# Tile 0's softmax in two parts of its keys, and the first three tiles' operations in one written list

## The chip, the cores and the metric

The kernel runs on one core of a Trainium2 chip. The metric is the device time of one execution, in microseconds (us). The engines work through queues of their own, in the order in which the program gives them work, and wait for each other by semaphores: PE (TensorE, matmuls), DVE (VectorE), ACT (ScalarE), POOL (GpSimd), and SP, whose queue issues every DMA here.

## The reference

```python
kv_pool = kv.reshape(B, H // r, r, W // r, r, C).mean(axis=(2, 4))   # r = 4
kv_flat = kv_pool.reshape(B, -1, C) @ w_sr                           # 768 keys, k = v
s = scale * (q @ k.transpose(0, 2, 1))
a = softmax(s)                       # over the keys, exp(s - max) / (sum + 1e-9)
x = a @ v                            # (B * 12288, 128)
h = x @ w_in                         # 128 -> 2048
out = gelu(h) @ w_out                # 2048 -> 128, gelu by erf
```

There are four batches (B) of 12,288 queries, C is 128, and q is eight times the usual draw. `w_in` and `w_out` come as 64-bit floats.

## The kernel before

The 49,152 queries are cut into 96 tiles of T = 512, 24 to a batch; a tile's queries are four chunks of 128. For a tile t the steps are:

- `q_load`, `q_max`, `q_scale`, `q_split` (or `q_halves`), `q_turn`: q is loaded, scaled by a power of two for each row, split into two f16 halves (upper and remainder), and transposed by DMA (`q_u` to `q_v`). `q_sigma` makes the factor `sg` that undoes the scale.
- `score`, `evac`, `exp`: for each chunk, six f16 matmuls of 384 columns give the 768 scores in PSUM (`s`, line 478); VectorE copies them out with the row's extreme (`sn`, line 489); ScalarE takes the exponential with its sum (line 540).
- `recips`, `attn_hi`, `attn_lo`, `attn_turn`: the reciprocal of the sum (`r`), the upper half and remainder of the normalized row (`a`, lines 561 and 565), and a DMA transpose (`aT`, line 574).
- `av`, `x_out`: 18 matmuls of 512 columns give x transposed (`px`, line 600), which VectorE splits into `xh` and `xl`.
- `mlp_in`, `gelu`, `rest`, `mlp_out`: 16 blocks of 128 of the hidden layer: three matmuls (`h`, lines 622 to 624), the gelu on ScalarE (`g`, line 635), its upper half for a pair of blocks on ScalarE (`gh`, line 637) and the remainder on VectorE (`gl`, line 643), three matmuls into `po` (lines 660 to 662). `ps_h`, with three PSUM banks, holds `h` and every small product.
- `o_turn`, `o_join`: the output is turned back by a DMA transpose between two copies on GpSimd, and stored.

Tile 0 is another matter: its keys, softmax and MLP are in f32, where one matmul instruction runs four passes. The first batch's key and value rows come in six parts (`kv_in`); VectorE adds neighbours twice (`kv_add`), a matmul with `pool32` pools and turns (`kv_pool`, `pp`), a matmul with `w_sr` gives the keys (`kv_key`, `pk`) and the values (`kv_nat`, `pv`). Its scores are two halves of 384 keys for each chunk (`score_half`, `evac_half`), but there is one exponential over all 768, one normalization (`norm`, line 445), six transposes on PE for a chunk (`a_turn`, `pa`) with their copies shared by ScalarE and VectorE (`a_evac`, line 461), and `av_pair`, 12 matmuls of 256 columns that give x transposed (`px`, line 586), copied by `x_first` into `x32`.

Beside this the weights are made ready: `w_load` brings 64-bit floats, `w_single` makes f32 of them by four integer passes, of which one is ScalarE's (line 719), `w_max` and `w_scale` find the scale (`rho`, `omega`; a product with `ones` spreads it over the partitions), and `w_half` writes f16 halves (`wi_h` and the like on ScalarE, line 784, `wi_l` and the like on VectorE, line 786).

The order on every engine is the order in which the code calls the steps (`tc.manual_schedule`). `START` is a list of calls, 52 lines long, for the preparation and tile 0, with the parts of tiles 1 and 2 that lie beside it. After it a loop over tile i and block f calls the steps of tiles i to i + 3 at fixed places, and `extra` puts the later batches' keys among them.

Of the kernel before, what the change touches and what calls it, by code (L numbers as in the profile page):

```python
# [20 lines left out]

START = [
    ("q_load", 0), ("w_sr",), ("kv_in", 0), ("kv_in", 1), ("kv_in", 2), ("kv_in", 3), ("kv_in", 4),
    ("kv_in", 5, 0, 2), ("kv_in", 5, 1, 2), ("q_load", 1), ("w_load", 0, 0, 2), ("w_load", 0, 1, 2),
    ("w_load", 1), ("w_load", 2), ("w_load", 3), ("q_load", 2),
    ("q_turn_first",),
    ("kv_add", 0), ("kv_pool", 0), ("kv_key", 0), ("kv_add", 1), ("kv_pool", 1), ("kv_key", 1),
    ("kv_add", 2), ("kv_pool", 2), ("kv_key", 2), ("kv_add", 3),
    ("score_half", 0, 0, 0), ("score_half", 0, 1, 0), ("kv_pool", 3), ("kv_key", 3),
    ("kv_max", 0), ("evac_half", 0, 0, 0), ("kv_add", 4),  # L30
    ("kv_pool", 4), ("score_half", 0, 2, 0), ("score_half", 0, 3, 0), ("kv_key", 4),
    ("evac_half", 0, 1, 0), ("kv_add", 5, 0, 2), ("kv_add", 5, 1, 2), ("kv_pool", 5), ("kv_key", 5),
    ("evac_half", 0, 2, 0), ("evac_half", 0, 3, 0), ("q_max", 1), ("q_scale", 1), ("q_halves", 1, 0),
    ("w_single", 0, 0), ("w_single", 0, 1), ("q_halves", 1, 1), ("q_turn", 1),
    ("score_half", 0, 0, 1), ("score_half", 0, 1, 1), ("score_half", 0, 2, 1),
    ("evac_half", 0, 0, 1), ("exp", 0, 0), ("score_half", 0, 3, 1),
    ("evac_half", 0, 1, 1), ("exp", 0, 1), ("kv_nat", 0),
    ("evac_half", 0, 2, 1), ("exp", 0, 2), ("recips", 0, 0, 1), ("norm", 0, "dve"),
    ("a_turn", 0, 0), ("a_turn", 0, 1), ("evac_half", 0, 3, 1), ("a_evac", 0, 0, "act"), ("exp", 0, 3),
    ("kv_max", 1), ("a_evac", 0, 1, "dve"), ("kv_bound", 0), ("kv_nat", 1),  # L40
    ("recips", 0, 1, 1), ("norm", 1, "dve"), ("kv_bound", 1), ("a_turn", 1, 0),
    ("a_turn", 1, 1), ("kv_bound", 2), ("a_evac", 1, 0, "act"), ("kv_high", 0), ("kv_high", 1), ("a_evac", 1, 1, "dve"),
    ("recips", 0, 2, 1), ("norm", 2, "dve"), ("av_pair", 0), ("a_turn", 2, 0), ("a_turn", 2, 1),
    ("kv_low", 0), ("a_evac", 2, 0, "act"), ("w_single", 1, 0),
# [34 lines left out]
def pooled_attention_mlp(  # L79
# [14 lines left out]
    nc = tc.nc  # L94
# [16 lines left out]
    LAG = 6  # L111

    GROUPS = H // P
    PARTS = 2 * GROUPS
    WL = 1024
# [76 lines left out]
    def kv_add(h, n=0, parts=1):  # L192


        v = st["row", h].rearrange("p (j w c) -> p j w c", w=R, c=C)
        v = v[:, n * 4 // parts : (n + 1) * 4 // parts]
        nc.vector.tensor_tensor(v[:, :, :2], v[:, :, :2], v[:, :, 2:], op=ALU.add)
        nc.vector.tensor_tensor(v[:, :, 0], v[:, :, 0], v[:, :, 1], op=ALU.add)

    def kv_pool(h):  # L200


        v = st["row", h].rearrange("p (j w c) -> p j w c", w=R, c=C)
        ps = ps_h.tile([P, T], F32, tag="ps_h", name=f"pp_{h}")
        for j in range(4):
            nc.tensor.matmul(  # L206
                ps[:, j * P // 4 : (j + 1) * P // 4], v[:, j, 0], pool32, start=True, stop=True
            )
        if h == 0:
            st["pT"] = ap_.tile([P, PARTS, P], F32, tag="a", name="pT")  # L210
        nc.scalar.copy(st["pT"][:, h], ps[:, :P])

    def kv_nat(n):


        if n == 0:
            st["v32"] = ap_.tile([P, KB, C], F32, tag="a", name="v32")
        ps = ps_h.tile([P, T], F32, tag="ps_h", name=f"pv_{n}")
        for k in range(3):
            nc.tensor.matmul(  # L220
                ps[:, k * C : (k + 1) * C], st["pT"][:, 3 * n + k], w_sr_sb, start=True, stop=True
            )
        nc.scalar.copy(
            st["v32"][:, 3 * n : 3 * n + 3].rearrange("p k c -> p (k c)"), ps[:, : 3 * C]
        )

    def kv_key_first(h):
        if h == 0:
            st["kT", 0] = prep.tile([P, KEYS], F32, tag="kT", name="kT_0")
        ps = ps_h.tile([P, T], F32, tag="ps_h", name=f"pk_{h}")  # L230
        nc.tensor.matmul(ps[:, :P], w_sr_sb, st["pT"][:, h], start=True, stop=True)
        nc.scalar.copy(st["kT", 0][:, h * P : (h + 1) * P], ps[:, :P])
# [138 lines left out]
    def q_max(t):  # L371

        st["qm", t] = small.tile([P, CH], F32, tag="qm", name=f"qm_{t}")
        nc.vector.tensor_reduce(
            st["qm", t], st["q", t], axis=AX.X, op=ALU.max, apply_absolute_value=True
        )

    def q_scale(t):

        m = st.pop(("qm", t))  # L380
        st["qe", t] = small.tile([P, CH], I32, tag="qe", name=f"qe_{t}")
        st["qi", t] = small.tile([P, CH], I32, tag="qi", name=f"qi_{t}")
# [17 lines left out]
    def q_halves(t, step):  # L400


        x = st["q", t]
        if step == 0:
            st["qu", t] = qs.tile([P, 2, CH, C], F16, tag="u", name=f"q_{t}_u")
        u, i = st["qu", t], st["qi", t].bitcast(F32)
        for c in range(CH):
            if step == 0:
                nc.scalar.mul(u[:, 0, c], x[:, c], i[:, c : c + 1])
            else:  # L410
                nc.vector.scalar_tensor_tensor(
                    u[:, 1, c], x[:, c], i[:, c : c + 1], u[:, 0, c],
                    op0=ALU.mult, op1=ALU.subtract,
                )
        if step == 1:
            del st["q", t], st["qi", t]
# [517 lines left out]
```

## Time and profile before

| what | value |
|---|---|
| runs | 2820.65, 2822.84, 2825.28 us (median 2822.84) |
| the profiled execution | 2821.22 us |
| its span on the core | 2819.5 us |
| PE, ACT, DVE, POOL busy | 2780.0, 2518.4, 2366.3, 847.0 us |
| mean granted TensorE clock | 0.997 |

A busy PE means that a matmul was under way, not that it ran at its peak. A row of groups has the number of instructions behind an x, then their busy time together in us and the mean of one in ns, and behind the second bar the idle time of the engine just before them and who ended it. A timeline row has the start, the time taken, the engine, the line, the operation, what it writes and reads, and in brackets the wait before it and its releaser. A window row has its bounds and length, then the busy time and the number of instructions for PE, its weight loads (PEld), DVE, ACT and POOL, the granted clock, the share of the DMA engines and GB/s. An f32 matmul shows as two records.

### The profile page before, as it was taken

What the parts mean: (1) busy time and instruction counts of PE and PEld (TensorE: products, weight loads), DVE (VectorE), ACT (ScalarE), POOL (GpSimd) and SP (SyncE); (2) the same over time, 40 slices, a digit from 0 to 9 for tenths busy, and PEclk for the clock granted to TensorE, in tenths of its full rate; (3) what the DMA queues carried; (4) which work ended last, traced back from release to release, by engine and by line L of the source; (5) the groups of instructions that cost most, each with busy time, mean ns of one, the idle gap of its engine ahead of it and who ended that gap; (6) DMA issues with size and microseconds to landing.
All of it is one profiled execution on the core that took longest, in us unless ns stands there. A gap on an engine that the chain in (4) does not pass through costs nothing.

```text
span 2819.5 us, 37507 instructions
## 1 busy us (share of the span) xinstructions
PE 2780.0 (99%) x13384; PEld 1329.3 (47%) x13384; DVE 2366.3 (84%) x3494; ACT 2518.4 (89%) x3411; POOL 847.0 (30%) x795
## 2 busy tenths in 40 slices
PE   7799999999999999999999999999999999999999
PEld 4344444444444444444444444444444444444444
DVE  7788888898888888888888888889888888888885
ACT  4699899999999999989999999999999989999997
POOL 0243442222243444222223434332322222222221
PEclk9899999999999999999999999999999999999999
DMA  5344543343445444434344444434443434343431
GB/s 184 89 103 113 118 112 90 94 99 92 96 103 122 109 108 102 98 86 103 90 97 120 107 106 106 111 92 93 97 96 89 93 90 97 90 97 90 95 90 48
DMA packets 844764, 283.05 MB, mean 100 GB/s; under 512 B 807200, under 2 KB 809632, under 8 KB 843808
## 3 DMA queue, kind: packets, MB, share of 16 engines
q1 hardware_dynamic: 844576, 280.65, 42.3%
q8 instruction: 105, 1.72, 0.3%
q14 instruction: 83, 0.68, 0.1%
HBM read 54.59 MB, written 25.17 MB: 28 GB/s over the span
## 4 chain that ended last, share of the span: by engine, by line
PE 95%; DVE 2%; ACT 1%; DMA 1%; POOL 1%; issue 1%; SPq 0%; DVEq 0%; ACTq 0%; POOLq 0%
PE s L478 13%; PE px L600 12%; PE po L661 11%; PE po L660 11%; PE po L662 11%; PE h L622 11%; PE h L624 11%; PE h L623 11%; DVE a L565 0%; PE po L654 0%; DMA q_v<-q_u 0%; DVE gl L643 0%; PE pp L206 0%; ACT sn L540 0%; DVE a L561 0%
## 5 line engine op out<-in xcount | busy, mean ns | idle before, releaser
L635 ACT ACTIVATE g<-h,hs 128x512 f32<-128x512 f32 x1520 | 995.3, 680 | 213.4 <-PE h L624 169.8
L643 DVE SCALAR_TENSOR_TENSOR gl<-g,gs,gh 128x1024 f16<-128x1024 f32 x760 | 1004.2, 1334 | 27.0 <-ACT gh L637 18.1
L637 ACT ACTIVATE gh<-g,gs 128x1024 f16<-128x1024 f32 x760 | 872.7, 1148 | 24.8
L660 PE MATMUL po<-gh,wo_h 128*128 128x512 f16 x1520 | 576.1, 379 | 1.7 <-ACT oT L667 1.7
L395 POOL TENSOR_TENSOR q<-q,qi 128x512 f32<-128x512 f32 x93 | 96.9, 1042 | 1599.7 <-DVE qi L387 1359.5
L661 PE MATMUL po<-gl,wo_h 128*128 128x512 f16 x1520 | 576.1, 379 | 0.4 <-DVE gl L643 0.4
L624 PE MATMUL h<-xh,wi_l 128*128 128x512 f16 x1520 | 576.3, 379 | 0.0
L623 PE MATMUL h<-xl,wi_h 128*128 128x512 f16 x1520 | 576.3, 379 | 0.0
L622 PE MATMUL h<-xh,wi_h 128*128 128x512 f16 x1520 | 576.3, 379 | 0.0
L662 PE MATMUL po<-gh,wo_l 128*128 128x512 f16 x1520 | 576.1, 379 | 0.0
L489 DVE TENSOR_SCALAR_CACHE_REDUCE sn<-s,sg 128x768 f32<-128x768 f32 x380 | 384.7, 1012 | 79.6 <-PE s L478 79.0
L478 PE MATMUL s<-k,q_v 128*128 128x384 f16 x2280 | 434.6, 327 | 14.3 <-DMA q_v<-q_u 7.5
L565 DVE SCALAR_TENSOR_TENSOR a<-sn,r,a 128x768 f16<-128x768 f32 x380 | 407.7, 1073 | 14.2 <-ACT a L561 0.8
L600 PE MATMUL px<-aT,v 128*128 128x512 f16 x1710 | 415.3, 379 | 0.0
L540 ACT ACTIVATE sn<-sn,nm 128x768 f32<-128x768 f32 x384 | 354.5, 924 | 1.2
L478 PEld LDWEIGHTS <-q_v 128*128 128x128 f16 x2280 | 223.3, 98 | 206.6 <-issue 13.0
L600 PEld LDWEIGHTS <-v 128*128 128x128 f16 x1710 | 167.3, 98 | 201.7
L561 DVE TENSOR_SCALAR a<-sn,r 128x768 f16<-128x768 f32 x378 | 248.4, 657 | 6.8 <-DVE r L557 0.3
L553 DVE TENSOR_SCALAR r<-sum 128x2 f32<-128x2 f32 (+1 forms) x193 | 40.8, 211 | 252.6 <-ACT sn L540 252.6
L369 POOL COPY o<-o_v 128x512 uint16<-128x512 uint16 x190 | 153.1, 849 | 279.0 <-DMA o_v<-o_u 273.3
L662 PEld LDWEIGHTS <-wo_l 128*128 128x128 f16 x1520 | 148.7, 98 | 180.0 <-issue 0.7
L624 PEld LDWEIGHTS <-wi_l 128*128 128x128 f16 x1520 | 148.8, 98 | 179.4 <-issue 0.3
(129 smaller groups left out, 2168.9 us busy)
## 6 DMA issues: line engine op xcount, KB each, us to landing
q<-in_q_dram SPq DMA_DIRECT2D x96, 256.0 KB, 2.9
out_dram<-o SPq DMA_DIRECT2D x95, 256.0 KB, 2.0
kv<-in_kv_dram SPq DMA_DIRECT2D x72, 256.0 KB, 4.4
aT<-a SPq DMA_TRANSPOSE x380, 3.2
row<-in_kv_dram SPq DMA_DIRECT2D x5, 1024.0 KB, 10.2
w<-in_moe_w_out_dram SPq DMA_DIRECT2D x2, 1024.0 KB, 10.8
q_v<-q_u SPq DMA_TRANSPOSE x95, 2.8
o_v<-o_u SPq DMA_TRANSPOSE x95, 2.7
```

The source lines that it names most:

```text
L478: nc.tensor.matmul(ps[:, n, :KH], lhs[:, c], rhs[:, n * KH : (n + 1) * KH], start=rhs is kh and lhs is qh, stop=lhs is ql,)
L565: nc.vector.scalar_tensor_tensor(a[:, 1, :], st.pop(("s", t, c)), st["r", t][:, c : c + 1], a[:, 0, :], op0=ALU.mult, op1=ALU.subtract,)
L600: nc.tensor.matmul(ps, v[:, w, :], aT[:, :, o + k, :], start=k == 0 and i == 0, stop=k == KB - 1 and i == 2,)
L622: nc.tensor.matmul(ps, wi_h[:, fs], xh, start=True, stop=False)
L623: nc.tensor.matmul(ps, wi_h[:, fs], xl, start=False, stop=False)
L624: nc.tensor.matmul(ps, wi_l[:, fs], xh, start=False, stop=True)
L635: nc.scalar.activation(g[:, e, :], ps, AF.Gelu, scale=st["hs", b] if t > 0 else 1.0)
L637: nc.scalar.mul(st["gh", t, f // 2], g, st["gs", b])
L643: nc.vector.scalar_tensor_tensor(gl, st["g", t, p], st["gs", t // TPB], st["gh", t, p], op0=ALU.mult, op1=ALU.subtract)
L660: nc.tensor.matmul(ps, wo_h[:, f, :], gh[:, e, :], start=f == 0, stop=False)
L661: nc.tensor.matmul(ps, wo_h[:, f, :], gl[:, e, :], start=False, stop=False)
L662: nc.tensor.matmul(ps, wo_l[:, f, :], gh[:, e, :], start=False, stop=f == FB - 1)
```

## The change

It has four parts.

1. **Tile 0's softmax.** Each chunk's keys are two parts, key blocks 0 to 2 and 3 to 5 (`CUT`). Each part has its own scores, maximum, exponential with sum, transposes and value product (`score_part`, `evac_part`, `exp_part`, `turn_part`, `turn_out_part`, `av_part`). `parts` makes the factors that bring both to a common maximum and sum, and `join_first` (ScalarE) and `join_second` (VectorE) apply them to the two products. The products have the queries on the partitions (24 matmuls of 128 columns), so `x_turn` turns x on PE afterwards.
2. **Work that changes engine.** For key parts 3, 4 and 5 VectorE's second addition is left out, and PE pools both columns (8 matmuls for 4). All copies of tile 0's transposes go to ScalarE. The scale of `w_out` is found by ScalarE as a sum of absolute values (`w_sum`) in place of VectorE's maximum. The upper halves of the weights go to VectorE, and most upper halves of `a` in tiles 1 to 3 to ScalarE.
3. **Smaller ones.** Tiles 1 and 2 have one scale for the four query rows of a partition (`JOINT`), so q's halves are one instruction each. `w_single`'s first step writes into `wa` itself.
4. **The list.** `START` now holds every operation of tiles 0, 1 and 2, and those of the tiles behind that lie among them; the loop starts at i = 3, through a generator `slots(i)` that yields the same steps in the old order.

```diff
+UNROLLED = 2
 START = [
-    ("q_load", 0), ("w_sr",), ("kv_in", 0), ("kv_in", 1), ("kv_in", 2), ("kv_in", 3), ("kv_in", 4),
...
+    ("q_load", 0), ("kv_in", 1), ("kv_add", 1), ("kv_in", 0), ("kv_in", 2), ("w_sr",),
...
+    JOINT = 2
+    SINGLE = (3, 4, 5)
+    CUT = (0, 3, KB)
...
         nc.vector.tensor_tensor(v[:, :, :2], v[:, :, :2], v[:, :, 2:], op=ALU.add)
-        nc.vector.tensor_tensor(v[:, :, 0], v[:, :, 0], v[:, :, 1], op=ALU.add)
+        if h not in SINGLE:
+            nc.vector.tensor_tensor(v[:, :, 0], v[:, :, 0], v[:, :, 1], op=ALU.add)
...
+        m = 2 if h in SINGLE else 1
         for j in range(4):
+            for w in range(m):
+                nc.tensor.matmul(
+                    ps[:, j * P // 4 : (j + 1) * P // 4], v[:, j, w], pool32,
+                    start=w == 0, stop=w == m - 1,
+                )
...
+    def evac_part(c, n):
...
+        ks = slice(CUT[n] * P, CUT[n + 1] * P)
+        nc.vector.tensor_scalar(
+            st["s", 0, c][:, ks], st.pop(("s0", c, n)), -SCALE, None,
+            op0=ALU.mult, op1=ALU.min, accum_out=st["nm0"][:, n, c : c + 1],
+        )
+    def exp_part(c, n):
+        s = st["s", 0, c][:, CUT[n] * P : CUT[n + 1] * P]
+        nc.scalar.activation(
+            s, s, AF.Exp, bias=st["nm0"][:, n, c : c + 1], scale=-1.0,
+            accum_out=st["sum0"][:, n, c : c + 1],
+        )
...
+    def av_part(c, n):
...
+        ps = st["x0", n, c // 2][:, c * C : (c + 1) * C]
+        for k in range(CUT[n], CUT[n + 1]):
+            nc.tensor.matmul(
+                ps, st["a0"][:, k, c * P : (c + 1) * P], st["v32"][:, k],
+                start=k == CUT[n], stop=k == CUT[n + 1] - 1,
+            )
+    def parts(step):
+        nm, sm, d, f = (st[x] for x in ("nm0", "sum0", "d0", "f0"))
+        if step == 0:
+            nc.vector.tensor_tensor(f[:, 0], nm[:, 0], nm[:, 1], op=ALU.min)
+            nc.vector.tensor_tensor(
+                d, f[:, 0:1].to_broadcast([P, 2, CH]), nm, op=ALU.subtract
+            )
+        if step == 1:
+            nc.scalar.activation(d, d, AF.Exp)
+        if step == 2:
+            nc.vector.tensor_tensor(f, sm, d, op=ALU.mult)
...
+    def join_first(c, mul):
...
+        mul(st["y0"][:, c], st["x0", 0, c // 2][:, c * C : (c + 1) * C], st["f0"][:, 0, c : c + 1])
+    def join_second(c):
+        y = st["y0"][:, c]
+        nc.vector.scalar_tensor_tensor(
+            y, st["x0", 1, c // 2][:, c * C : (c + 1) * C], st["f0"][:, 1, c : c + 1], y,
+            op0=ALU.mult, op1=ALU.add,
+        )
...
-            nc.scalar.mul(st["wy", j], up.bitcast(F32), DOWN)
+            nc.scalar.mul(a, up.bitcast(F32), DOWN)
...
+    def w_sum(j):
...
+        nc.scalar.activation(
+            wo_hf[:, k * WL : (k + 1) * WL], wa[:, j * WL : (j + 1) * WL], AF.Abs,
+            accum_out=st["wm", i][:, k : k + 1],
+        )
...
-        for i in range(1, NT + 1):
...
+        for i in range(UNROLLED + 1, NT + 1):
+            for name, *a in slots(i):
+                by[name](*a)
```

Three places show how the order moves. The first is VectorE at the evacuation of tile 2's first scores, `sn_2_0`. (`w_3` and `w_0` are pieces of the raw weights, `wa` the f32 weights, `a_1_2` chunk 2 of tile 1's normalized rows.) Before:

```order
L557 RECIPROCAL r_1_554<-r_1_554 128x2
L721 TENSOR_SCALAR w_3_162<-w_3_162 128x1024
L565 SCALAR_TENSOR_TENSOR a_1_2_576<-sn_1_2_472,r_1_554,a_1_2_576 128x768
L565 SCALAR_TENSOR_TENSOR a_1_3_581<-sn_1_3_502,r_1_554,a_1_3_581 128x768
L723 SCALAR_TENSOR_TENSOR w_3_162<-w_3_162 128x1024
L727 SCALAR_TENSOR_TENSOR wa_134<-wy_3_477,w_3_162 128x1024
L489 TENSOR_SCALAR sn_2_0_605,nm_2_603<-s_2_0_596,sg_2_529 128x768
L489 TENSOR_SCALAR sn_2_1_618,nm_2_603<-s_2_1_611,sg_2_529 128x768
```

After:

```order
L834 TENSOR_SCALAR w_1_436<-w_1_436 128x1024
L836 SCALAR_TENSOR_TENSOR w_2_426<-w_2_426 128x1024
L504 TENSOR_SCALAR sg_2_519<-qe_2_279,ks_0_324 128x1
L676 TENSOR_SCALAR r_1_521<-sum_1_405 128x2
L679 RECIPROCAL r_1_521<-r_1_521 128x2
L659 TENSOR_SCALAR sn_2_0_526,nm_2_524<-s_2_0_494,sg_2_519 128x768
L849 TENSOR_REDUCE wm_0_544<-wa_134 128x1
L840 SCALAR_TENSOR_TENSOR wa_134<-wa_134,w_2_426 128x1024
L687 SCALAR_TENSOR_TENSOR a_1_0_534<-sn_1_0_406,r_1_521,a_1_0_534 128x768
```

Tile 2's first evacuation moves ahead of all of tile 1's normalization, and the weights' passes lie between it and the next.

The second is SP's queue at the transposes of q and of the normalized rows. Before:

```order
L329 DMA_TRANSPOSE v_0_394<-k_0_361 128x12x128
L421 DMA_TRANSPOSE q_2_v_527<-q_2_u_486 128x8x128
L348 DMA q_3_531<-in_q_dram 128x512
L574 DMA_TRANSPOSE aT_1_560<-a_1_0_557 128x12x128
L574 DMA_TRANSPOSE aT_1_560<-a_1_1_564 128x12x128
L574 DMA_TRANSPOSE aT_1_560<-a_1_2_576 128x12x128
L574 DMA_TRANSPOSE aT_1_560<-a_1_3_581 128x12x128
L421 DMA_TRANSPOSE q_3_v_706<-q_3_u_702 128x8x128
```

After:

```order
L400 DMA_TRANSPOSE v_0_430<-k_0_350 128x12x128
L817 DMA w_1_436<-in_moe_w_in_dram 128x2048
L495 DMA_TRANSPOSE q_2_v_482<-q_2_u_290 128x8x128
L821 DMA w_3_509<-in_moe_w_out_dram 128x8x256
L419 DMA q_4_532<-in_q_dram 128x512
L696 DMA_TRANSPOSE aT_1_584<-a_1_0_534 128x12x128
L495 DMA_TRANSPOSE q_3_v_616<-q_3_u_580 128x8x128
L696 DMA_TRANSPOSE aT_1_584<-a_1_1_554 128x12x128
L696 DMA_TRANSPOSE aT_1_584<-a_1_3_604 128x12x128
```

Tile 3's q moves ahead of three of tile 1's transposes, and two loads of weights, which stood ahead of `v_0`, move behind it.

The third is ScalarE around tile 0's x (`x32`, the input of `h_0_0`). Before:

```order
L317 ACTIVATE k_0_361<-kT_0_182,kinv_0_354 128x384 x2
L461 COPY aT_0_314<-pa_2_0_375 128x3x128
L719 ACTIVATE wy_1_385<-w_1_158 128x1024
L469 COPY x32_391<-px_0_0_368 128x256
L461 COPY aT_0_314<-pa_3_0_396 128x3x128
L635 ACT_TABLE_LOAD
L635 ACTIVATE g_0_0_421<-h_0_0_419 128x512
L635 ACTIVATE g_0_0_421<-h_0_1_426 128x512
```

After:

```order
L832 ACTIVATE wa_134<-w_2_426 128x1024
L617 ACTIVATE y0_417<-xa_346,f0_221 128x128
L832 ACTIVATE wa_134<-w_1_436 128x1024
L617 ACTIVATE y0_417<-xa_346,f0_221 128x128
L667 ACTIVATE sn_1_1_420,sum_1_405<-sn_1_1_420,nm_1_404 128x768
L667 ACTIVATE sn_1_0_406,sum_1_405<-sn_1_0_406,nm_1_404 128x768
L636 COPY x32_489<-px_0_0_479 128x256
L636 COPY x32_489<-px_0_1_491 128x256
L667 ACTIVATE sn_1_2_447,sum_1_405<-sn_1_2_447,nm_1_404 128x768
L741 ACT_TABLE_LOAD
L741 ACTIVATE g_0_0_514<-h_0_0_502 128x512
```

Passes over weights, joins and two of tile 1's exponentials now stand ahead of the copy of x, and a third exponential behind it, ahead of the first gelu.

More of the change, by code (lines that the diff above doesn't have):

```diff
@@ L426, in q_sigma @@
     def q_sigma(t):
-        st["sg", t] = small.tile([P, CH], F32, tag="sg", name=f"sg_{t}")
+        n = 1 if t <= JOINT else CH
+        st["sg", t] = small.tile([P, CH], F32, tag="sg", name=f"sg_{t}")[:, :n]
         nc.vector.tensor_scalar_mul(
@@ new lines, in score_part @@
+    def score_part(c, n):
+        name = f"s0_{c}_{n}"
+        if c < 2:
+            if ("ps0", n) not in st:
+                st["ps0", n] = ps_s.tile([P, 2, 512], F32, tag="ps_s", name=name)
+            ps = st["ps0", n][:, c]
+        elif n == 0:
+            pool, tag = ((ps_o, "ps_o"), (ps_t, "ps_t"))[c - 2]
+            ps = pool.tile([P, T], F32, tag=tag, name=name)
+        else:
+            ps = ps_h.tile([P, T], F32, tag="ps_h", name=name)
+        ks = slice(CUT[n] * P, CUT[n + 1] * P)
+        ps = ps[:, : ks.stop - ks.start]
+        nc.tensor.matmul(ps, st["q32"][:, c], st["kT", 0][:, ks], start=True, stop=True)
+        st["s0", c, n] = ps
@@ new lines, in evac_part @@
+    def evac_part(c, n):
+        if "nm0" not in st:
+            for x in ("nm0", "sum0", "d0", "f0"):
+                st[x] = small.tile([P, 2, CH], F32, tag=x, bufs=1, name=x)
+        if ("s", 0, c) not in st:
+            st["s", 0, c] = sp.tile([P, KEYS], F32, tag="s", name=f"sn_0_{c}")
+        ks = slice(CUT[n] * P, CUT[n + 1] * P)
+        nc.vector.tensor_scalar(
+            st["s", 0, c][:, ks], st.pop(("s0", c, n)), -SCALE, None,
+            op0=ALU.mult, op1=ALU.min, accum_out=st["nm0"][:, n, c : c + 1],
+        )
@@ L452, in attn_turn_first, with turn_part @@
+    def exp_part(c, n):
[4 more added lines that the diff above has]
+        )
+    def turn_part(c, n):
+        if "a0" not in st:
+            st["a0"] = atp.tile([P, KB, T], F32, tag="aT", name="aT_0")
         ps = ps_h.tile([P, T], F32, tag="ps_h", name=f"pa_{c}_{n}")
-        for k in range(3):
+        for k in range(CUT[n], CUT[n + 1]):
+            o = (k - CUT[n]) * P
@@ L466, in x_first @@
-    def x_first(n, copy=nc.scalar.copy):
-        if n == 0:
+            st["a0"][:, CUT[n] : CUT[n + 1], c * P : (c + 1) * P],
+            st.pop(("pa", c, n))[:, :w].rearrange("p (k t) -> p k t", t=P),
+        )
+    def av_part(c, n):
+        if n == 0 and ("x0", 0, 0) not in st:
+            st["x0", 0, 0] = ps_x.tile([P, T], F32, tag="ps_x", name="xa")
+            st["x0", 0, 1] = st["x0", 0, 0]
+        if ("x0", n, c // 2) not in st:
+            pool, tag = ((ps_t, "ps_t"), (ps_o, "ps_o"))[c // 2]
+            st["x0", 1, c // 2] = pool.tile([P, T], F32, tag=tag, name=f"xb_{c}")
+        ps = st["x0", n, c // 2][:, c * C : (c + 1) * C]
+        for k in range(CUT[n], CUT[n + 1]):
+            nc.tensor.matmul(
+                ps, st["a0"][:, k, c * P : (c + 1) * P], st["v32"][:, k],
+                start=k == CUT[n], stop=k == CUT[n + 1] - 1,
+            )
@@ L543, in exp @@
         )
-    def exps(t):
-        for c in range(CH):
-            exp(t, c)
     def recips(t, c=0, n=CH):
@@ L738, in w_max @@
             apply_absolute_value=True,
+        )
+    def w_sum(j):
+        i, k = j // NW, j % NW
+        if ("wm", i) not in st:
+            st["wm", i] = small.tile([P, NW], F32, tag=f"wm{i}", name=f"wm_{i}")
+        nc.scalar.activation(
+            wo_hf[:, k * WL : (k + 1) * WL], wa[:, j * WL : (j + 1) * WL], AF.Abs,
+            accum_out=st["wm", i][:, k : k + 1],
         )
```

604 lines of the change are left out of this document (323 added, 281 removed).

## The prediction

> **What bounds the kernel now.** I read the page's busy table and slices first, then the busy time by stretch, the timeline of the first 125 us, and the groups there for durations. All times are us from the start of the span.
>
> ```profile
> span 2819.5 us, 37507 instructions
> PE 2780.0 (99%) x13384; PEld 1329.3 (47%) x13384; DVE 2366.3 (84%) x3494; ACT 2518.4 (89%) x3411; POOL 847.0 (30%) x795
> PE   7799999999999999999999999999999999999999
> ```
>
> Only the first two slices (141 us) are not full on PE: no later edit of order can win much, and the change touches only the head. By stretch:
>
> ```profile
> 0.00:45.70 45.70, 30.51 (x143) 23.89 (x143) 30.57 (x74) 17.08 (x38) 1.33 (x10) 1.00 0.76 263
> 45.70:121.04 75.34, 58.24 (x204) 26.91 (x205) 57.85 (x104) 43.38 (x64) 8.37 (x8) 0.89 0.31 70
> 45.70:68.30 22.60, 21.79 (x70) 10.17 (x70) 19.16 (x44) 13.98 (x24) 0.00 (x0) 1.00 0.10 24
> 104.60:121.60 17.00, 17.00 (x74) 8.02 (x73) 14.87 (x19) 12.69 (x17) 6.13 (x5) 1.00 0.61 133
> 121.60:150.31 28.71, 28.27 (x138) 13.31 (x136) 27.09 (x37) 25.86 (x35) 14.11 (x13) 1.00 0.43 92
> 150.31:207.65 57.34, 57.34 (x280) 27.47 (x279) 49.76 (x75) 52.37 (x71) 24.27 (x23) 1.00 0.48 111
> ```
>
> The columns are PE, PEld, DVE, ACT and POOL busy. From 150.31 to 207.65 PE is busy all the time: two tiles in 57.34, and ACT, the next, at 52.37 (91%). From 45.7 to 121.04 PE is idle for 17.1 of 75.3. Where that idle lies, with the first add, the last key's copy and my two marks:
>
> ```profile
> 7.94 1.22 DVE L197 TENSOR_TENSOR row<-row 128x1024 f32<-128x1024 f32 x1 [7.94 <-DMA row<-in_kv_dram]
> 27.93 0.27 ACT L232 COPY kT<-pk 128x128 f32<-128x128 f32 x1 [0.58 <-PE pk L231]
> 45.69 1.98 PE L619 MATMUL h<-x,wa 128*128 128x512 f32 x4 [0.52 <-DVE ks L311]
> 47.52 1.14 PE L478 MATMUL s<-k,q_v 128*128 128x384 f16 x6
> 70.41 1.13 PE L619 MATMUL h<-x,wa 128*128 128x512 f32 x2 [2.07 <-ACT g L635]
> 77.52 2.08 PE L478 MATMUL s<-k,q_v 128*128 128x384 f16 x6 [5.98 <-DVE sn L489]
> 79.39 1.61 PE L654 MATMUL po<-g,wa 128*128 128x512 f32 x2
> 92.91 0.46 PE L283 MATMUL omega_ps<-omega_d,ones 128*128 128x128 f32 x2 [1.78 <-DVE omega_d L277]
> 97.08 1.23 SPq L421 DMA_TRANSPOSE q_v<-q_u  x1
> 99.83 2.10 PE L478 MATMUL s<-k,q_v 128*128 128x384 f16 x6 [6.46 <-DMA q_v<-q_u]
> 121.04 1.46 PE L600 MATMUL px<-aT,v 128*128 128x512 f16 x6
> ```
>
> The first mark is 45.69, where tile 0's MLP starts. The second, which I call M, is 121.04: tile 2's first value matmul. The brackets are waits: for a gelu behind the table loads (2.07), for VectorE's evacuation of tile 2's first scores (5.98), for the weights' scale (1.78), and for tile 3's q, transposed after it was split late (6.46). After the two long waits a score block takes 2.08 and 2.10 instead of 1.14, and a tile-0 matmul 1.61 instead of about 1.0: a cold restart costs some 1.5. Six matmuls of 512 columns take 1.46 and six of 384 take 1.14, so 128 columns cost 0.053, a score matmul 0.16 and one of 512 0.215. Durations I use:
>
> ```profile
> L540 ACT ACTIVATE sn<-sn,nm 128x768 f32<-128x768 f32 x14 | 13.0, 926 | 0.1
> L540 ACT ACTIVATION_READ_ACCUMULATOR sn<-sn,nm 128x1 f32 x14 | 2.6, 188 | 0.0
> L540 ACT ACT_TABLE_LOAD x3 | 3.8, 1283 | 0.1
> L561 ACT ACTIVATE a<-sn,r 128x768 f16<-128x768 f32 x2 | 1.9, 928 | 0.5 <-DVE r L557 0.5
> L461 ACT COPY aT<-pa 128x384 f32<-128x384 f32 x4 | 1.9, 477 | 3.3 <-PE pa L454 3.3
> L719 ACT ACTIVATE wy<-w 128x1024 f32<-128x1024 f32 x4 | 4.6, 1140 | 2.1 <-PE po L654 2.1
> L489 DVE TENSOR_SCALAR_CACHE_REDUCE sn<-s,sg 128x768 f32<-128x768 f32 x12 | 12.1, 1011 | 6.6 <-PE s L478 6.5
> L445 DVE TENSOR_SCALAR sn<-sn,r 128x768 f32<-128x768 f32 x4 | 2.5, 620 | 0.1
> L461 DVE COPY aT<-pa 128x384 f32<-128x384 f32 x4 | 2.2, 553 | 0.9 <-PE pa L454 0.8
> L736 DVE TENSOR_REDUCE wm<-wa 128x1 f32<-128x1024 f32 x4 | 4.8, 1213 | 0.0
> L198 DVE TENSOR_TENSOR row<-row 128x512 f32<-128x512 f32 x5 | 3.5, 692 | 0.2
> L561 DVE TENSOR_SCALAR a<-sn,r 128x768 f16<-128x768 f32 x6 | 3.7, 615 | 0.1
> L411 DVE SCALAR_TENSOR_TENSOR q_u<-q,qi,q_u 128x128 f16<-128x128 f32 x8 | 2.4, 348 | 0.1
> L206 PE MATMUL pp<-pool,row 128*128 128x32 f32 x48 | 8.8, 340 | 5.2 <-DVE row L198 5.2
> L586 PE MATMUL px<-aT,v 128*128 128x256 f32 x24 | 5.7, 388 | 1.4 <-ACT aT L461 1.4
> L220 PE MATMUL pv<-w_sr_sb,pT 128*128 128x128 f32 x12 | 1.8, 284 | 0.0
> w<-in_moe_w_out_dram SPq DMA_DIRECT2D x2, 1024.0 KB, 10.8
> ```
>
> **The change, part one: up to tile 0's x.** The keys come in by the same DMAs in another order; the last part still ends the chain. Parts 3 to 5 lose VectorE's second add (0.69, 0.42 for a half part) and take 12 more pool matmuls on PE (8.8/24 = 0.37 each, 4.4 in all); on the last part that is a trade of about equals, hidden for the others behind the DMAs, at most 0.5 late if not. The gain from the two parts is that tile 0's exponentials and transposes of the first three key blocks run while the last keys load. But behind the last key ScalarE now has six half exponentials (0.46 and 0.19 each, 3.9), eight copies of transposes (3.8, four of them from VectorE), three conversions of weights that used to come partly later (3.4), two exponentials of tile 1 (2.2), the joins (four of about 0.27), the two k halves (1.2), x32 (0.7) and small ones (1.3): some 17.6. The last key is copied at 28.2 before; I put it at 29.5, since the last part's pooling doubles and ScalarE has four other copies around it. With 3 of waits that puts x at about 50, 4 to 5 later than 45.7. By then PE has done five score blocks of tiles 1 and 2 (5 × 6 × 0.16 = 4.8) that came behind the mark before. So this stage by itself is worth nothing, or +1 to −1. The 24 value matmuls of 128 columns (1.8/6 = 0.30 each, 7.3 against 12 of 0.48, 5.7) and four transposes lie where PE is idle for 4 of 17 and are covered. The w loads move behind q_1's and the values' transposes on SP's queue: w_1 goes out at about 37 and has to be there at 46; if it took the 10.8 of the row under full load, ScalarE would be 1.5 late, else nothing.
>
> **Part two: VectorE up to M.** VectorE feeds every wait of the list above, so I date M by its queue. Before, it was busy for 30.57 + 57.85 = 88.4 by M, and not busy for 121.04 − 7.94 − 88.4 = 24.7. Taken out ahead of M: four normalizations (2.5), four copies (2.2), one x copy (0.4), second adds (2.2), two weight maxima, which go to ScalarE (2.4), small ones of the old softmax (1.5), four of six upper halves of a, which go to ScalarE (2.5), q's eight pieces in two (1.3), work that now comes behind M (1.9): 16.9. Put in: two evacuations more (2.2), upper halves of all four weights (0.615 × 1024/768 = 0.82, 3.3), four joins (1.4), two copies (0.5), a dozen small ones of 0.17 (2.0): 9.4. Net −7.5: 81 busy.
>
> How long it stands idle is the unknown. Where it was well supplied it was busy for 19.16 of 22.60 and 14.87 of 17.00; at the better share 81 take 92.6, that is 11.6 idle. At worst it is starved as before: 24.7. In the new order tile 2's scores are evacuated between pieces of weight work and directly behind r, tile 3's q is split and on SP's queue before three of tile 1's transposes, and the weights' scale is asked of PE only behind a score block, so each of the four waits has lost its cause: I take 17, a little nearer the supplied end. M is then 7.5 (one small DMA less ahead of the first keys) + 81 + 17 + 2 (a score block and three matmuls between VectorE's last evacuation and the values) = 107.5; the ends are 102 and 115.
>
> Crosscheck from PE: of the 17.1 idle and some 4 of cold pace between the marks, 13.5 and the 3.2 below would go, and 4.5 of new waits be left. ScalarE's queue up to M is fuller too (nine table loads for six, eight upper halves of a for two, six passes over weights for eight), but still idle for some 10.
>
> **Part three: behind M.** PE has two score blocks (12 matmuls) and six matmuls of 512 more done by M: 12 × 0.16 + 6 × 0.215 = 3.2 less is left. ScalarE gets a table load pair more often in tiles 1 to 3 (two loads in all, 2.6) and holds one upper half of a more; with 91% use in the steady state it has little room, so I add 2.5 of PE waiting, between 0 and 5. From tile 3 on the order is the old one.
>
> Sum, against the profiled execution's own 2821.2 (span 2819.5): 2821.2 − 13.5 − 3.2 + 2.5 = 2807. The runs' median, 2822.8, stands 1.6 above that execution; between the two footings I name 2808. Ends: M at 102 and nothing behind it, 2799; M at 115 and 5 behind it, 2817, or 2819 by the median.
>
> [...]
>
> ```profile
> 61.23 1.09 ACT L635 ACTIVATE g<-h 128x512 f32<-128x512 f32 x2 [1.18 <-PE po L654]
> 62.33 1.28 ACT L540 ACT_TABLE_LOAD   x1
> 63.63 0.93 ACT L540 ACTIVATE sn<-sn,nm 128x768 f32<-128x768 f32 x1
> ```
>
> Here a load starts 0.01 after the gelu's end and the exponential 0.02 after the load: a switch costs 1.28. [...]
>
> **Rivals.**
> - The queues starve as before (0.11). For it: VectorE's idle of 24.7 came in many places, not only at four waits, and a list written out over three tiles fixes the order where durations slip. M at 115 to 118 and 5 behind it: 2817 to 2822, no change. Against: ahead of the four waits the new order has other work for PE.
> - A switch of tables holds ScalarE for as long again (0.02): three more ahead of M, 3.8, 2811. Against it the rows above.
> - Transposes come late (0.08): tile 3's a is finished by VectorE only after its tile-2 x and four gelu remainders, and its two last transposes go out just ahead of their use. A wait like 6.46 and a cold restart of 1.5: 2815.
> - Slower (0.05): ScalarE holds tile 0's gelus back. Between gelus it now has three blocks of loads, exponentials and halves: 2 × 1.28 + 3 × 1.11 = 5.9, 2 × 1.28 + 2 × 1.11 + 2 × 0.93 = 6.6, and 0.93 + 2 × 1.28 + 2 × 1.11 = 5.7. PE has three banks for h; if nothing else covered, it would wait 18.2, with three cold restarts 22.7: 2830. It decides only if all three go bare; with two it is no change. Against: before, a block of 8.1 (two loads, four exponentials, one weight half) cost PE 2.07.
>
> **Chances.** Forecast, 2800 to 2815: 0.72; still faster: 0.02; the others as given. Of changes under 0.2% (5.6 us, about what these runs can tell) a measurement says little. Faster by more, that is below 2817: 0.72 + 0.02 + 0.02, most of the late transposes (0.07) and a little of the starved case (0.02): 0.85. Within: 0.10. Slower: 0.05. The range 2800 to 2819 holds the forecast's ends and leaves out half the starved case, the slower one and what is faster still, some 0.15.
>
> **What would show it.** Tile 0's MLP starting at about 50, with PE busy through; no wait above 3 for an evacuation or a transposed q between 50 and M; M (tile 2's first value matmul) at 102 to 115; 81 busy on VectorE by then; three more table loads on ScalarE ahead of it. Wrong would be: M past 117, a PE wait above 5 on ScalarE's gelus, or tiles 1 to 4 taking over 29.5 each behind M.

## The result and the profile after

| what | before | after |
|---|---|---|
| median of the runs | 2822.14 us (2820.65 to 2825.28, 4 runs) | 2796.59 us (2795.89 to 2796.96, 4 runs) |
| span of the profiled execution | 2819.5 us | 2794.2 us |
| tile 0's x / M (tile 2's first value matmul) | 45.69 / 121.04 | 48.27 / 100.94 |
| tile 5's first value matmul | 207.48 | 183.53 |

The ratio is 0.9908 [0.9891, 0.9925]: 25.5 us faster, where 14 were forecast. The direction and the place (the head of the kernel) were right; the time lies below the forecast's range. The page of the changed kernel: span, busy time by engine, PE's slices, and the shares of the chain that ended last.

```profile
span 2794.2 us, 37612 instructions
PE 2778.3 (99%) x13436; PEld 1333.6 (48%) x13436; DVE 2351.9 (84%) x3472; ACT 2525.5 (90%) x3430; POOL 854.2 (31%) x795
PE   8999999999999999999999999999999999999999
PE 99%; ACT 0%; DVE 0%; DMA 0%; issue 0%; SPq 0%; ACTq 0%; DVEq 0%
```

PE's work is what it was (2778.3 for 2780.0), and only the first slice is still not full. By stretch (length, then PE, PEld, DVE, ACT, POOL busy, granted clock, DMA share, GB/s): up to M, from x to M, and from M to tile 5's values.

```profile
0.00:100.94 100.94, 90.88 (x416) 56.53 (x417) 82.68 (x171) 70.58 (x126) 19.82 (x23) 0.98 0.59 177
48.27:100.94 52.67, 52.31 (x192) 24.49 (x193) 51.59 (x97) 47.89 (x70) 18.49 (x13) 1.00 0.43 100
100.94:183.53 82.59, 82.59 (x400) 39.20 (x399) 69.40 (x96) 76.02 (x102) 33.69 (x30) 1.00 0.44 103
```

The stretch from x to M was 75.35, with PE idle for 17.1 of it and VectorE for 17.5. Now it is 52.67, with PE idle for 0.36 and VectorE for 1.08: both queues are full. PE's waits behind its start, over the whole span, and then the timeline's rows of the first addition, the last key's copy and the marks:

```profile
PE po L768 <- ACT oT L777: 1.7, 2, 1.1
PE s L536 <- DVE sn L546: 0.7, 1, 0.7
PE pt L796 <- ACT oT L779: 0.6, 1, 0.6
PE s L648 <- DVE sn L659: 0.4, 1, 0.4
PE px L629 <- DVE y L621: 0.3, 1, 0.3
PE h L728 <- ACT x L636: 0.2, 1, 0.2
```

```profile
6.33 1.23 DVE L252 TENSOR_TENSOR row<-row 128x1024 f32<-128x1024 f32 x1 [6.33 <-DMA row<-in_kv_dram]
28.25 0.27 ACT L303 COPY kT<-pk 128x128 f32<-128x128 f32 x1 [0.16 <-PE pk L299]
48.27 1.98 PE L728 MATMUL h<-x,wa 128*128 128x512 f32 x4 [0.22 <-ACT x L636]
95.75 1.14 PE L648 MATMUL s<-k,q_v 128*128 128x384 f16 x6 [0.36 <-DVE sn L659]
100.94 1.46 PE L707 MATMUL px<-aT,v 128*128 128x512 f16 x6
183.53 1.46 PE L707 MATMUL px<-aT,v 128*128 128x512 f16 x6
```

Of the four waits of before (2.07, 5.98, 1.78 and 6.46) only the fourth row is left, 0.36 for an evacuation; the second, fifth and sixth belong to tile 0's own chain up to x, and `po` and `pt` wait at the very end, as they did. Between 48.27 and 95.75 PE waits for nothing that the view lists.

### The profile page after: what moved, and what is told of

Its sections match the earlier page's. It is cut to its first block, busy times and chain, and to the rows that moved or that the text cites. A ratio compares the mean times of both kernels' runs of the same rounds, so it can differ in the third digit from the quotient of the medians.

```text
span 2794.2 us, 37612 instructions
## 1 busy us (share of the span) xinstructions
PE 2778.3 (99%) x13436; PEld 1333.6 (48%) x13436; DVE 2351.9 (84%) x3472; ACT 2525.5 (90%) x3430; POOL 854.2 (31%) x795
## 3 DMA queue, kind: packets, MB, share of 16 engines
q8 instruction: 105, 1.72, 0.3%
## 4 chain that ended last, share of the span: by engine, by line
PE 99%; ACT 0%; DVE 0%; DMA 0%; issue 0%; SPq 0%; ACTq 0%; DVEq 0%
PE px L707 13%; PE s L648 13%; PE po L768 12%; PE po L770 12%; PE po L769 12%; PE h L731 12%; PE h L733 12%; PE h L732 12%; PE h L728 1%; PE po L762 0%; PE pp L264 0%; PE s L536 0%; DMA row<-in_kv_dram 0%; PE pk L333 0%; ACT g L741 0%
## 5 line engine op out<-in xcount | busy, mean ns | idle before, releaser
L683 DVE TENSOR_SCALAR a<-sn,r 128x768 f16<-128x768 f32 x371 | 242.6, 654 | 7.1 <-DVE r L679 0.8
L676 DVE TENSOR_SCALAR r<-sum 128x2 f32<-128x2 f32 x189 | 39.4, 208 | 245.0 <-ACT sn L667 245.0
```

## The experiments

All but two start from the changed kernel, whose time is taken as 2796.2 to 2796.6; the kernel before has medians from 2822.1 to 2828.1 beside them. An arrow stands for the length from x to M in the profile, of which each kernel has one. An edit to the list is shown by its calls alone, taken out of longer lines.

**The changed kernel again, and the full queues.**

> The changed kernel once more, as the footing for the three that run with it: 2796.6 by its four runs, from 2795.9 to 2797.0. A difference of under 1 between it and an experiment is taken for none.

2796.21 us. x came at 49.38 and M at 102.06, → 52.68: x moves by 1 from one execution to the next, the stretch does not.

```diff
+    def hold(kind):
+        k = st["kT", 0]
+        if kind == "dve":
+            t = small.tile([P, 1], F32, tag="hold", bufs=1, name="hold")
+            nc.vector.tensor_reduce(t, k, axis=AX.X, op=ALU.max, apply_absolute_value=True)
...
-    ("gelu", 0, 2), ("q_sigma", 2),
+    ("gelu", 0, 2), ("hold", "dve"), ("q_sigma", 2),
...
```

> Four maxima over 128x768 f32, some 0.95 each (a 128x384 maximum took 0.55), are added to VectorE's queue at four places between tile 0's x and M, tile 2's first value matmul: 3.8 of work whose result nobody reads. Theory V (the prediction's: VectorE's queue dates M; it was busy for 51.59 of the 52.67 between the two): M at 104.7 and the time 3.8 later, 2800.4. Theory P (PE's own work is the bound from x on, it was busy for 52.31 of 52.67, and VectorE runs ahead of it): as long as VectorE's lead on PE is over 3.8 nothing, 2796.6 to 2797.6; PE shows no new wait above 1.

```diff
-    ("w_single", 3, 1),
-    ("w_single", 3, 2),
-    ("w_single", 3, 3),
...
+        n = 8 if j == 1 else WL
-            st["wm", i][:, k : k + 1], wa[:, j * WL : (j + 1) * WL], axis=AX.X, op=ALU.max,
+            st["wm", i][:, k : k + 1], wa[:, j * WL : j * WL + n], axis=AX.X, op=ALU.max,
```

> The last quarter of w_out is left as ScalarE's first pass makes it (three passes of VectorE over 128x1024 left out, 0.69 + 1.22 + 1.22), and the maximum of w_in's second half goes over 8 columns instead of 1024 (1.1 less): 4.2 less on VectorE between x and M, and the output's last bits of weights are wrong by that. Theory V: M at 96.7, the time 4.2 less, 2792.4. Theory P: no change, 2796.1 to 2797.0, and M at 100.9.

```diff
-    ("mlp_out", 0, 2),
...
-    ("mlp_out", 0, 6),
```

> Five of tile 0's sixteen second-layer products (blocks 2 to 6, one f32 matmul of 512 columns each, four passes of 0.215: 0.86) are left out, so tile 0's output lacks them: 4.3 less on PE between x and M, nothing changed for VectorE and ScalarE. Theory P: M at 96.6, the time 4.3 less, 2792.3, VectorE now the fuller engine of the stretch. Theory V: PE waits for VectorE in the place of the work left out, M at 100 to 101 and the time 2796 to 2797.

Rows of x to M: more on VectorE, less on VectorE, less on PE.

```profile
47.84:105.52 57.68, 54.49 (x191) 24.79 (x192) 55.41 (x101) 48.14 (x70) 17.62 (x13) 0.97 0.43 91
47.79:100.33 52.54, 52.17 (x192) 24.49 (x192) 46.60 (x94) 47.89 (x70) 16.81 (x13) 1.00 0.42 100
48.29:100.94 52.65, 48.55 (x181) 22.44 (x182) 51.56 (x97) 47.68 (x70) 18.47 (x13) 1.00 0.43 100
```

2800.91 us, 2795.47 us and 2795.82 us. VectorE's added work came through whole (→ +5.0 for 3.8, with a PE wait of 2.46 for an evacuation and a granted clock of 0.97 in the row), so theory P, that VectorE runs ahead, falls. But taking 5 off VectorE shortened the stretch by 0.13, and taking 3.8 off PE by 0.02: theory V falls too as far as it says that VectorE alone holds the stretch. With less on PE, new waits stand in the place of the work left out:

```profile
61.03 2.93 PE L728 MATMUL h<-x,wa 128*128 128x512 f32 x6 [1.67 <-ACT g L741]
69.42 1.14 PE L648 MATMUL s<-k,q_v 128*128 128x384 f16 x6 [1.92 <-DVE sn L659]
```

**Both at once** (the two edits together):

> The two lighter kernels in one: 4.2 less on VectorE and 4.3 less on PE between x and M, with the same parts of the output left out. Each by itself left the stretch at 52.5 to 52.7. Theory B (the two queues are filled to the same height): now both are shorter, M 3.5 to 4.2 earlier, the time 2792 to 2793. Theory C (neither queue dates M, but a chain through both and ScalarE, which is busy for 47.9 of the 52.7): M stays within 1, 2795 to 2797.

```profile
48.59:98.87 50.28, 48.24 (x182) 22.47 (x183) 47.07 (x94) 47.69 (x70) 16.80 (x13) 1.00 0.45 105
```

2793.87 us, → 2.4 shorter: between the two theories. Neither queue gives anything alone; together they give about half of what they lost, so the list has PE and VectorE at nearly the same height. What holds the other half was not shown: ScalarE is then nearly as full, at 47.69 of 50.28, but no run took work off it alone, and a chain of waits through all three engines (theory C) would fit as well.

**The moved work put back.**

```diff
-    SINGLE = (3, 4, 5)
+    SINGLE = ()
-    ("turn_out_part", 0, 1, "act"),
+    ("turn_out_part", 0, 1, "dve"),
...
-    ("w_hi", 0, "dve"),
+    ("w_hi", 0, "act"),
...
-    ("w_sum", 2),
+    ("w_max", 2),
...
-    ("attn_hi", 1, 0, "act"),
+    ("attn_hi", 1, 0, "dve"),
...
```

> The work that changed engine goes back under the new list: the second additions of parts 3 to 5 on VectorE (+2.2 there, 12 f32 pool matmuls off PE), half of the copies of tile 0's transposes on VectorE (+2.2), w_out's scale by two maxima on VectorE (+2.4), six upper halves of a in tiles 1 to 3 on VectorE (+3.7), the weights' upper halves on ScalarE (-3.3 on VectorE): +7.2 on VectorE by M, -7 on ScalarE. Theory B with VectorE as one of the two full queues: M 6 to 7 later and the time 2802 to 2804. Rival L (the list alone makes the gain, and the moved work is spare): 2795 to 2798.

2810.87 us: 14.5 of the gain are gone, twice the sum of VectorE's work, and 11.6 against the kernel before are left. x at 52.70 (+4.4), → 62.94 (+10.3). Two kernels split it: the additions (`SINGLE`) alone, and everything from `w_hi` on.

> The second additions of key parts 3 to 5 alone go back to VectorE (0.69, 0.69 and 2 x 0.42) and 12 f32 pool matmuls leave PE; all else as in the changed kernel. With all the moved work back x was at 52.70, 4.4 later. If these additions made that, the loading stage is held by VectorE: x at 50 to 52 and the time 2799 to 2801. Rival: PE's 12 matmuls (0.23 each there) were worth about as much, x within 1 and the time 2796 to 2797; the 4.4 then belong to the copies of the transposes.

2796.73 us, x at 49.12: nothing beyond the 1 by which x moves anyhow. Alone, the additions were no part of the gain. The 4.4 of x then come from the copies, or from the two together; that wasn't separated.

> Only what changed engine behind the loading of the keys goes back: w_out's scale by two maxima on VectorE (+2.4), six upper halves of a on VectorE (+3.7), the weights' upper halves on ScalarE (-3.3 on VectorE). By the sum of VectorE's work M is 2.8 later and the time 2799 to 2800. Rival (the list fits these engines alone, and a step on another engine makes waits of its own): x to M as long as with all of it back, 62.9 against 52.7, and the time 2806 to 2807.

2807.34 us, → 63.38: 10.7 longer, for 2.8 of VectorE's work by the sum. Its parts, first the weights' upper halves alone:

> Of the changed kernel's moved steps only the four upper halves of the weights go back to ScalarE: 3.3 less on VectorE, 4.5 more on ScalarE. By the sum of VectorE's work M is not later, the time 2793 to 2797. Theory K (the step on VectorE spares a crossing: ScalarE's half waits for the scale, VectorE's remainder for the half, and exponentials queue behind the halves): VectorE waits 2 to 3 for the half and 2 for the next sum as with all of it back, PE 3 to 4 and a cold block behind it, x to M 57 to 60 and the time 2801 to 2804.

2803.56 us, → 58.92, with less work on VectorE than in the changed kernel:

```profile
47.79:106.71 58.92, 53.33 (x191) 24.25 (x192) 47.93 (x92) 51.26 (x73) 17.52 (x12) 1.00 0.38 89
70.80 0.16 DVE L883 RECIPROCAL inv<-rho 128x1 f32<-128x1 f32 x1
73.70 1.28 DVE L914 SCALAR_TENSOR_TENSOR wi_l<-wa,inv,wi_h 128x1024 f16<-128x1024 f32 x1 [2.55 <-ACT wi_h L908]
76.96 0.17 DVE L676 TENSOR_SCALAR r<-sum 128x4 f32<-128x4 f32 x1 [1.98 <-ACT sn L667]
```

In the changed kernel VectorE makes scale, halves and remainder without a stop, and meets the next sum on time:

```profile
71.54 1.41 DVE L908 TENSOR_SCALAR wi_h<-wa,inv 128x1024 f16<-128x1024 f32 x2
72.99 1.28 DVE L914 SCALAR_TENSOR_TENSOR wi_l<-wa,inv,wi_h 128x1024 f16<-128x1024 f32 x1
74.35 0.17 DVE L676 TENSOR_SCALAR r<-sum 128x4 f32<-128x4 f32 x1
```

The waits are those of theory K: where ScalarE makes the half, VectorE waits 2.55 for it and 1.98 for the exponentials that queue behind it. VectorE's idle time from x to M is 58.92 − 47.93 = 11.0, where the changed kernel has 1.1: 3.7 of VectorE's time buys 6.2. ScalarE also has 3.4 more to do in the stretch, and PE waits 3.5 for gelus in it; how much of the 6.2 is the crossing and how much ScalarE's load was not separated. And the rest:

> The rest of that: w_out's scale by two maxima on VectorE (+2.4) and six upper halves of a on VectorE (+3.7), the weights' upper halves stay on VectorE. By the sum M is 6.1 later, the time 2802 to 2803. Theory K: the crossing made most of the 10.7, and here VectorE has no wait for ScalarE; of the 6.1 at most that comes through, 2800 to 2803. If hi_back costs nothing, this one has to cost 10, 2806.

2801.52 us, → 57.47, 4.8 longer for 6.1 of work by the sum, of which 5.0 lie ahead of M: nearly all of that comes through, and VectorE is idle for 0.9. The two parts, 6.2 and 4.8, make 11.0, where both together made 10.7.

```profile
48.90:106.37 57.47, 53.41 (x191) 24.19 (x192) 56.57 (x104) 42.78 (x61) 17.89 (x12) 1.00 0.39 92
```

**Tile 0's parts without the overlap** (the first part's calls moved behind `("kv_key_out", 5, "act")`):

> The first part's four scores, evacuations and exponentials wait behind the last key's copy, so that no part of tile 0's softmax lies beside the loading of the keys any more; all else as in the changed kernel. If that overlap is worth something: PE has four scores of 0.64 (2.6), VectorE four evacuations of 0.56 (2.2) and ScalarE two exponentials of 0.62 (1.2) more between 28.3 and x, x 2.5 to 4 later and the time 2799 to 2801. Rival: that stretch is held by ScalarE or the chain of the second part, x at 48 to 49 and the time 2796 to 2797.

2802.89 us; x at 54.49 (+6.2, more than either expected), M at 107.15, → 52.66 as ever. The last key was copied at 30.70 for 28.25, so 2.5 of the 6.2 lie ahead of it and 3.8, within the 2.5 to 4 expected, behind it. The 2.5 go with PE's pace: with no score between, the pooling stayed at half pace to the end (48 records in 10.45, where 32 took 3.65). That the missing scores are the reason fits the runs on the pace below, but was not tried by itself.

**Order alone in the kernel before.**

```diff
-    ("w_scale", 1, 1), ("q_max", 3), ("q_scale", 3), ("q_split", 3), ("q_turn", 3), ("q_sigma", 3),
+    ("evac", 2, 2), ("q_max", 3), ("q_scale", 3), ("q_split", 3), ("q_turn", 3), ("q_sigma", 3),
```

> The kernel before, with one move in its list: tile 3's q is scaled, split and transposed behind tile 2's third evacuation, where VectorE was idle for 2.86, instead of behind tile 0's last gelu. Theory O (the kernel before was held by its four waits, each of which falls to order alone): the wait of 6.46 and its cold score block of 1 go, 2814 to 2816. Theory B: VectorE's work by M is the same and what waited was PE, which was not full there; VectorE's queue was held up for 2.97 and 1.36 behind that wait, so 3 to 4 at most come back, 2818 to 2819.

2820.02 us (2814.57 to 2823.61, 10 runs) against 2822.50 (13 runs): a ratio of 0.9984 [0.9973, 0.9996]. The time is 2.5 lower, a little less than either theory had. → 71.99, 3.4 shorter, as in theory B: the 6.46 is gone, and 1.64 for gelus, 0.39 for an evacuation and 1.55 for a transpose of `a` stand in the same stretch. Undoing one wait did not bring its length. The 3.4 rests on one profile each; in the last run of this section, whose list behind x is that of the kernel before, the stretch took 77.29 in place of 75.35. But x came at 52.00, for 45.69 in the profile before, with nothing changed ahead of it.

**PE's pace while the keys load.** Matmul rows of the kernel before, then of that last one. A score matmul is two records. Half pace means that like matmuls take about twice the time, as the last rows show (2.85 and 5.49):

```profile
18.79 2.92 PE L511 MATMUL s<-kT,q 128*128 128x384 f32 x4 [0.35 <-ACT kT L232]
23.66 0.98 PE L206 MATMUL pp<-pool,row 128*128 128x32 f32 x8
28.25 2.85 PE L511 MATMUL s<-kT,q 128*128 128x384 f32 x8 [0.36 <-ACT kT L232]
```

```profile
19.24 2.92 PE L511 MATMUL s<-kT,q 128*128 128x384 f32 x4 [0.36 <-ACT kT L232]
24.66 1.75 PE L206 MATMUL pp<-pool,row 128*128 128x32 f32 x8
32.62 5.49 PE L511 MATMUL s<-kT,q 128*128 128x384 f32 x8 [0.36 <-ACT kT L232]
```

The same two score matmuls brought the full pace by 23.66 in one execution and not in the other. Four kernels work on that; the first two put products of a constant with 128 columns into PE's gaps, the others such with 512. `("warm", 16)` or `("dense", 5)` stands at the head of the changed kernel's list, and in the second and third kernel `("warm", 2)` or `("dense", 1)` ahead of each of the five `kv_pool` behind the first; the fourth is the kernel before, with `("dense", 2)` behind `("score_half", 0, 1, 0)`.

```diff
+    def warm(n):
...
+        for k in range(n):
+            nc.tensor.matmul(ps[:, :P], ones, ones, start=True, stop=True)
...
+    def dense(n):
...
+        for k in range(n):
+            nc.tensor.matmul(
+                ps, ones, ones.unsqueeze(1).to_broadcast([P, CH, P]), start=True, stop=True
+            )
```

> 16 f32 products of a constant with itself (128 columns, into a bank nobody reads) stand ahead of everything on PE, where it is idle until 8.4. In all these profiles the first matmuls run at half pace (a score matmul of tile 0 1.46 where it takes 0.75 later, eight records of pooling 1.76 for 0.98) up to 18 to 37 us from the start. Theory H (the half pace of PE holds the loading stage): the full pace is there at 8.4, the last key's copy 2 to 4 earlier than 28.3, the time 2792 to 2795. Rival (the keys' DMAs and VectorE hold that stage, or the sparse pool matmuls bring the half pace back at once): 2796 to 2797.

2795.87 us, x at 48.29: no gain. The full pace was there at the first pooling and gone by the third:

```profile
8.48 1.05 PE L269 MATMUL pp<-pool,row 128*128 128x32 f32 x8 [0.92 <-issue]
13.49 1.89 PE L269 MATMUL pp<-pool,row 128*128 128x32 f32 x8 [1.19 <-issue]
```

> The same, with two more of these products (0.31 each at full pace) ahead of each pooling from the second on, to hold the full pace through the loading stage, the granted clock of 0.50 to 0.75 at 26 to 31 included. Theory H: the time 2791 to 2794, below the other. Rival: the ten added products cost PE 3 in a stage where it is full, 2797 to 2800.

2796.13 us (2795.27 to 2799.78): x at 47.31 in the profile, no gain in the runs.

> [...] If the half pace came back for want of busy columns: pooling takes 1.0 for eight records in all of the stage, x at 44 to 46, and the time 2793 to 2795. Rival: the five products cost PE what the pace gives, x at 48 to 49 and 2796 to 2797.

2794.06 us (2793.85 to 2794.52): 2.1 below the changed kernel's 2796.2, and their runs don't overlap, though they were taken on different chips. All of the pooling is at full pace (1.05 to 1.08 for eight records, 1.87 for sixteen), x comes at 46.28, M at 98.92, → 52.64:

```profile
13.31 1.08 PE L272 MATMUL pp<-pool,row 128*128 128x32 f32 x8 [0.29 <-DVE row L255]
24.55 1.87 PE L272 MATMUL pp<-pool,row 128*128 128x32 f32 x16
46.28 5.68 PE L736 MATMUL h<-x,wa 128*128 128x512 f32 x12 [0.24 <-ACT x L644]
```

> The kernel before with two such products behind tile 0's first two score matmuls, so that PE is densely busy there for 5 to 6 instead of 2.9. If the time at which the full pace comes makes the kernel before vary (2819.8 to 2829.3 in its runs), it comes at about 23 in every run: x at 45 to 47, the time 2820 to 2823 with a spread under 3. Rival: no difference to the kernel before in median or spread.

2825.25 us, ratio 0.9998 [0.9989, 1.0008]. The spread fell (3.4 in 10 runs, against 11.2 in 13 of the kernel before beside it), the median did not: the two products waited 1.72 for their bank and took 3.47 on the path, and x came at 50.57. That the kernel before varies by the time at which the full pace comes fits this; its cost in the median is not shown.

## Why the prediction was wrong

- **What bounds it: right.** The head alone changed, and PE's work with it hardly.
- **What dates M: half right.** The forecast dated M by VectorE's queue alone. More work there does lengthen the stretch (+5.0 for 3.8), but 5 less shortened it by 0.13, since PE's queue is now as full.
- **Up to x: near.** x at 48.27 (about 50 forecast), the last key's copy at 28.25 (29.5). The five score blocks forecast, 4.8, are done ahead of x, and x is only 2.6 later than before: the stage won 2.2 where the forecast had nothing, 1.6 of it by the earlier first addition.
- **VectorE's work by M: right.** 82.68 for 81.
- **VectorE's idle time: the step that failed.** The forecast took 17 between ends of 11.6 and 24.7, and 2 more behind VectorE's last evacuation; the trace has 100.94 − 6.33 − 82.68 = 11.9 for both. M came at 100.94, below the end of 102: 6.6 ahead of 107.5, by 7.1 less of idle time and a start 1.2 earlier, against 1.7 more work. The forecast said that each of the four waits had lost its cause, and still kept 5.4 of waiting above the supplied end.
- **The scale behind it: near the mark by luck.** The "better share", 87.5%, is almost the share that came from the first addition to M (82.68 of 94.61, 87.4%), but only because two errors cancel. Ahead of x VectorE's idle time grew, from 7.2 to 48.27 − 6.33 − 31.10 = 10.8; from x to M it fell from 17.5 to 1.1, and there VectorE is busy for 51.59 of 52.67, 98%. The share was no bound: in the window that gave it VectorE still waited 1.87 for a gelu's upper half from ScalarE. The same rows held a better mark for x to M, seen only afterwards: PE was busy for 58.24 there; less the 4 of cold pace (an estimate of the forecast's) and the 4.8 of score blocks done ahead of x, and with the 3.2 more done ahead of M, that is 52.6, and the stretch took 52.67.

```profile
0.00:48.27 48.27, 38.58 (x225) 32.03 (x225) 31.10 (x75) 22.69 (x57) 1.33 (x10) 0.96 0.77 261
```

- **Why it was so small: shown in part.** Under the new list a step that the forecast's sum had as a loss (upper halves of the weights, +3.3 on VectorE) is a gain: put back alone it makes 10 of idle time on VectorE and M comes 5.8 later, while what else was moved behind x, put back without it, makes none. But this is not what VectorE had waited for before. There ScalarE made the halves too, and the remainders started without a wait, in an order that had other work between; VectorE's longest waits from x to M were 6.5 in all for scores from PE, 3.4 for sums from ScalarE and 2.9 for x transposed from PE:

```profile
69.18 1.28 DVE L786 SCALAR_TENSOR_TENSOR wi_l<-wa,inv,wi_h 128x1024 f16<-128x1024 f32 x1
80.57 1.28 DVE L786 SCALAR_TENSOR_TENSOR wi_l<-wa,inv,wi_h 128x1024 f16<-128x1024 f32 x1
102.91 2.47 DVE L786 SCALAR_TENSOR_TENSOR wo_l<-wa,inv,wo_h 128x1024 f16<-128x1024 f32 x2
DVE sn L489 <- PE s L478: 6.5, 4, 3.0
DVE xh L610 <- PE px L600: 2.9, 1, 2.9
```

So the order and the engines work together: the list fits these engines. What the order is worth by itself stays open; it was tried with one move in the kernel before (2.5), and with all the moved work put back, together with tile 0's parts and under a list that was written for other engines (11.6).

- **Behind M: the 2.5 was not there.** PE is busy for all of 82.59. From M to tile 5's values it took 86.44 before, so 3.85 came: the 3.2 of work done ahead of M, which was right, and 0.65.
- **Table loads:** two more ahead of M (8 for 6), not three, and no PE wait for a gelu. Each takes 1.28 in both traces, and between x and M the next operation starts 0.01 to 0.02 behind it.
- **The rest:** the remaining 1.35 of the spans' 25.3 (20.1 + 3.85 + 1.35) lies behind tile 5's values, where the trace of before had a late wait of 1.0 for a transposed q that is absent here. Of the 11.1 by which the profiled time lies below the sum's 2807, 6.6 are thus M, 2.5 and 0.65 the stretch behind it, and 1.35 this.
- **Rivals:** none came. The four waits went, tile 3's transposes were on time, and ScalarE's blocks were covered.

## What to carry to other kernels

When idle time is the unknown, don't scale it from a stretch that itself waits: take each engine's own work through the stretch, and let the fullest one give the early end. A short step that stands between two others of one engine is worth trying on that engine, even if it is full: under this list, moving it away freed 3.7 and cost 6.2. And where two engines are filled to the same height, taking work off one of them shows nothing (here 0.13 and 0.02), which does not mean that it is spare.

## What the runs showed of the hardware

In these runs PE starts at half pace: eight records of the pooling with 32 columns take 1.75 to 1.89, and 0.97 to 1.08 at the full pace. The full one shows only behind a stretch of wider matmuls: in the changed kernel 3.34 of scores with 384 columns, with products of a constant at its head 6.36 of those with 128 columns or 6.47 of those with 512. One stretch of 2.92 of two score matmuls brought it in one execution and not in another with the same list up to x: it was there by 23.66 in the one (the kernel before), and the other shows it first at 37.90 (six records with 128 columns in 0.97, which took 1.65 at half pace in the changed kernel). What makes that difference no run here shows.

The changed kernel's pooling stayed at half pace from 8.4 to the score matmuls at 17.7, though the profile shows PE as busy almost without a gap (19.77 of 19.87 up to the last key); the same pooling lost the full pace within about 5 us where it had been given (1.05 at 8.48, then 1.89 at 13.49), and kept it with one product of 512 columns ahead of each part behind the first (1.05, then 1.08 at 13.31). In the changed kernel the column of the granted clock read 1.00 in every window of 3 to 6 from 8 to 26, at either pace, so here the pace is read from the durations of like matmuls.

```profile
8.38:28.25 19.87, 19.77 (x104) 17.61 (x105) 12.84 (x28) 5.07 (x16) 0.00 (x0) 0.97 0.99 350
```

A matmul of 512 columns took 0.86 from start to start in f32 and 0.215 in f16 (85.12 to 85.98 and 85.98 to 86.41, two of them, in the changed kernel): four passes stand in this case for four times the time.
